# Retention and a hard-swish MLP on one core: first Q in float32 by two queues, Q columns by parity, row order in the stores, moved tile steps

## The chip, the core and the metric

The kernel runs on one core of a Trainium2 chip. The core has five engines that run their own instruction streams and wait for each other by semaphores: TensorE (PE; its weight loads are shown apart, as PEld), VectorE (DVE), ScalarE (ACT), GpSimd (POOL) and SyncE (SP). Transfers between HBM and SBUF run on 16 DMA engines; POOL, SP and ACT issue them. The metric is device time in microseconds of one execution. Before the change it is 287.6 us (median of 3 runs, 287.4 to 288.43).

## The reference

Inputs q, k, v are float32 of shape (8 batches, 8 heads, 576 tokens, 64); w_in is 512 x 2048, w_out 2048 x 512. What is computed:

```python
scores = q @ k.T / sqrt(64)                    # per batch and head
gamma  = 1 - 2 ** (-5 - h)                     # per head
D[i,j] = gamma ** (i - j) if i >= j else 0
attn   = (scores * D) @ v                      # (8, 8, 576, 64)
x      = attn as (8 * 576 tokens, 512)
h      = x @ w_in
g      = h * clip(h + 3, 0, 6) / 6
out    = g @ w_out                             # (4608, 512) float32
```

## The kernel before

Matrix products take float16 and give float32 in PSUM; loads by POOL cast float32 to float16 on the way.

The 4608 tokens are worked as 9 blocks `kb` of 512 columns. A block's columns are four pieces of 128 tokens. Pieces are ordered by position first: pieces 0 to 7 are the first 128 tokens of the eight batches, pieces 8 to 15 the next 128, and so on up to piece 31; pieces 32 to 35 hold the last 64 tokens of two batches each. So blocks 0 and 1 are all first pieces, which have no state from earlier tokens.

Pieces 0 to 7 are worked two at a time as tiles t = 0 to 3 (`first_load`, `turned`, `first_scores`, `first_out`, `first_copies`, `first_states`; L118 to L329). `first_load` puts two neighbouring tokens on one partition: partition p of a half (one batch each) holds tokens 2p and 2p+1, index `w`. `turned` transposes Q or K per parity `w` and head pair on TensorE against an identity and copies PSUM to SBUF. In the copy for Q it puts the columns back into the order of the tokens, by a strided pattern; keys stay by parity. `first_scores` multiplies K by Q, and its `mask` multiplies by `decay`, a table of decay factors made from `gap` and `behind` (L142 to L175). `first_out` multiplies with V; the result is copied to `xt`, the block's 512 columns. `first_scale` and `first_states` make the state that the next pieces of the same batch start from. All of that is called in pieces: tiles 0 and 1 at the start, 2 and 3 between the matmuls of block 0's GEMM2 and block 1's GEMM1.

Later pieces (`step4`, L757) use a running state. Their Q and K are scaled by `ahead` (L331) on DVE and then transposed by a DMA transpose that SP issues; scores of pieces 8 and 9 are the first that need one (`put_step(1, (-1, -1), [], groups[0])`, ahead of block 1's GEMM2).

Each block then has GEMM1 (`g1`, `g1_pair`: 16 chunks of 128 hidden columns, ACT and DVE apply the activation) and GEMM2. Blocks 0 and 1 use the plain form `g2` in 16 units (row group `mc`, a quarter of the sum `part`); when a row group is complete ACT copies it to `osb` and `store` (L512) sends 128 rows of 512 float32 with SP. In block 0 the order of units is by `part` first, so its four stores come close together at the end; in block 1 by `mc` first, so they are spread. Blocks 2 to 8 use `g2_seven`, seven half-size products from sums of weights (`weight_sums`, `t1` to `t4`) and sums of activations.

The order on every engine is the order in which the program is written out: no scheduler moves instructions. `put(units, steps)` runs numbered units and after unit j the steps listed under j. `load_next` issues one third (K, Q or V) of a later piece on POOL and makes it wait for the newest matmul recorded in `newest`. `warm` issues float32 matmuls on zeros in places where TensorE waits. PSUM has four shared banks (`bank`, tag `ph`) and the tags `sc`, `o` and `tu`.

SP's queue carries, in order: four stores of block 0, the transposes of pieces 8 to 13, four stores of block 1 with transposes among them, and so on.

Of the kernel before, what the change touches and what calls it, by code (L numbers as in the profile page):

```python
# [13 lines left out]
ALU = mybir.AluOpType  # L14
# [3 lines left out]
def kernel(  # L18
# [98 lines left out]

    def first_load(t, x):  # L118
        dst = first_of(t, x)
        for i in range(2):  # L120
            nc.gpsimd.dma_start(  # L121
                dst[i * HALF:i * HALF + HALF].rearrange("p h w d -> p h (w d)"),
                (q, k, v)[x][2 * t + i, :, 0:P, :].rearrange("h (p w) d -> p h (w d)", w=2))
# [10 lines left out]
    def load_wout(c0, c1):  # L134
# [31 lines left out]
    behind = const.tile([P, 2, P], FP32)  # L166
    nc.vector.tensor_scalar(out=behind, in0=gap, scalar1=0.0, scalar2=1e5, op0=ALU.is_lt,
                            op1=ALU.mult)
    nc.vector.tensor_tensor(out=behind, in0=behind, in1=gap, op=ALU.add)

# [41 lines left out]
    def warm(n, cols):  # L212

        w = psum.tile([P, MBLK], FP32, tag="tu", name=f"warm_{warmed[0]}")
# [5 lines left out]
    warm(4, MBLK // 2)  # L220

# [23 lines left out]
    def turned(t, x, copy, tag=None, ws=(0, 1)):  # L245


        src, n = first_of(t, x), len(ws)
        pt = bank_or(tag, [P, n, NPAIR, P], FP16, f"tr{'qk'[x]}_{t}_{ws[0]}")
        for i, w in enumerate(ws):  # L250
            for p in range(NPAIR):
                for h2 in range(2):
                    newest[0] = nc.tensor.transpose(pt[rows(h2), i, p, :],
                                                    src[:, 2 * p + h2, w, :], ident16)
        if x not in fst.setdefault(t, {}):
            fst[t][x] = work.tile([P, 2, NPAIR, P], FP16, tag="qk", bufs=8, name=f"t{'qk'[x]}_{t}")
        to = fst[t][x]
        if x:
            copy(to[:, ws[0]:ws[0] + n], pt)
        else:  # L260
            copy(to.rearrange("d a b c -> d (a b c)").rearrange("d (u s w) -> d w u s", w=2, s=HALF),
                 pt.rearrange("d w p (i s) -> d w (p i) s", i=2))

    def first_scores(t, w, tags=()):
        kt = fst[t][1]
        qt = fst[t][0].rearrange("d a b c -> d (a b c)").rearrange("d (p i s) -> d p i s",
                                                                   p=NPAIR, i=2)
        if tags:
# [7 lines left out]
        for p in range(NPAIR):  # L276
            for i in range(2):
                for h2 in range(2):
                    nc.tensor.matmul(banks[h2][rows(i), p, :], kt[rows(h2), w, p, rows(i)],
                                     qt[rows(h2), p, i, :], start=True, stop=True)  # L280

        def mask():
            if tags:
                for h2 in range(2):
                    nc.vector.tensor_tensor(out=at[:, h2], in0=banks[h2], in1=decay[:, w, h2],
                                            op=ALU.mult)
            else:
                nc.vector.tensor_tensor(out=at, in0=sc, in1=decay[:, w], op=ALU.mult)
# [223 lines left out]
    def store(kb, mc, cols, src):  # L512
        if kb < B:
            _, b, i, _ = pieces[PER * kb + mc]
            r0 = b * S + i * P
            nc.sync.dma_start(out[r0:r0 + P, cols], src)
        else:
# [7 lines left out]
    def g2(kb, mc, part):  # L525
# [4 lines left out]
        for fc in range(4 * part, 4 * part + 4):  # L530
            nc.tensor.matmul(pout, gt[:, fc, P * mc:P * mc + P], wout16[:, fc, :],  # L531
                             start=(fc == 0), stop=(fc == NFC - 1))
        if part == 3:
# [153 lines left out]
    for i in range(2, 4):  # L687
        load_win(i * WQ, i * WQ + WQ)
    for i in range(4):
        load_wout(4 * i, 4 * i + 4)  # L690
        if i > 1:
            for x in range(3):
                first_load(i, x)
# [7 lines left out]
    warm(1, 160)  # L701
    first_scores(0, 0)()
    turned(1, 0, by_act)
    first_scores(0, 1, (None, None))()
    warm(1, 160)
    turned(1, 1, by_act, ws=(0,))
    turned(1, 1, by_act, ws=(1,))
    warm(1, MBLK // 2)
# [94 lines left out]
    def gemm1(kb, steps):  # L803

        units = [lambda fc=fc, cols=cols: g1_pair(kb, fc, cols)
                 for cols in (lo, hi) for fc in {2: (0, 2)}.get(kb, ())]
        done = {0: 4, 1: 14, 2: 4}.get(kb, 0)
        if kb < 2:

            units = [lambda fc=fc: g1_pair(kb, fc, hi) for fc in range(0, done, 2)]  # L810
        put(units + [unit1(kb, f) for f in range(done, NFC)], steps)

    load_until(11)
    gemm1(0, {3: [(powers,)], 5: [(fill_gk2,)], 7: [(first_scale, 0), (fill_gqk, 1)],
              9: [(fill_gqk, 0)], 11: [(first_scale, 1)]})
    order = [(mc, part) for part in range(4) for mc in range(4)]
# [5 lines left out]
    def scores_of(t):  # L824
# [6 lines left out]
        {3: [(first_states, 0, 1)], 4: [(weight_sums, "t1")], 5: [(make_mask64,)],  # L831
         7: [(begin, 2), (first_scale, 2)], 10: [(scores_of, 2)], 11: [(weight_sums, "t2")],
         13: [(first_out, 2), (first_copies, 2, (by_act, by_act)),
              (weight_sums, "t3")],
         14: [(begin, 3)]})

    for fc in range(0, 14, 2):
        g1_pair(1, fc, lo)
        if fc == 0:
            scores_of(3)  # L840
        if fc == 4:
            ahead(8)
        if fc == 8:
            first_out(3)
            first_copies(3, (by_act, by_act))
            ahead(9)
            first_states(2)
        if fc > 8:
# [3 lines left out]

    within = {0: [(ahead, 10)], 4: [(ahead, 11)]}
    for j in (0, 2, 3, 5, 7, 8):
# [5 lines left out]
    groups = [[c, c + 1] for c in range(8, NP, 2)]  # L860
    steps_at = {1: {-1: [(ahead, 12)],
                    7: [(weight_sums, "t4")]}}

# [76 lines left out]
```

## Time and profile before

| | |
|---|---|
| Median of 3 runs | 287.6 us |
| Profiled execution | 287.82 us |
| Its span (first to last instruction) | 286.0 us |
| TensorE busy | 278.2 us, 97% |
| DVE busy | 228.4 us, 80% |
| ACT busy | 170.6 us, 60% |
| POOL busy | 104.3 us, 36% |
| Granted TensorE clock | 1.0 throughout |
| DMA moved | 35.72 MB, mean 125 GB/s |

How to read it: the profile is of one execution on the chip. A line of the time line gives start, duration, engine, line of the program, operation, what is written and read, and in square brackets how long the engine was idle before and what ended that. "L469" is line 469 of the kernel. A line of an answer for one source line or tile gives durations in ns as least, median and most. "DMA to landing" is the time from the issue to the last byte's semaphore. A DMA queue's line gives packets, MB, and the time its packets took as a share of 16 engines' time; q0 is POOL's queue, q1 SP's. A part that was idle on an engine that is not the bound costs nothing.

### The profile page before, as it was taken

To read this page: it belongs to the slowest core of one execution; us is meant where nothing else is said; L and a number is where in the kernel's file an instruction comes from. 1 tells how busy PE (TensorE), PEld (TensorE's weight loads), DVE (VectorE), ACT (ScalarE), POOL (GpSimd) and SP (SyncE) were. 2 spreads that over 40 slices of the span, in tenths; PEclk is the share of its full clock that TensorE was granted. 3 is DMA by queue.
4 is the path that set the end of the run, shared out by engine and by line. 5 is a ranking of instruction groups with operands and counts; after the bars stand their busy time and mean duration, and the time that the engine had idled before them with its cause. 6 is when DMAs were issued, how large, how long until landed. Compare 5 with 4: busy or idle time off the path is not lost.

```text
span 286.0 us, 9020 instructions
## 1 busy us (share of the span) xinstructions
PE 278.2 (97%) x3836; PEld 183.4 (64%) x3836; DVE 228.4 (80%) x385; ACT 170.6 (60%) x295; POOL 104.3 (36%) x136
## 2 busy tenths in 40 slices
PE   6999999999999999999999999999999999999994
PEld 4674455874465687468745974597458845874583
DVE  4577656999769998899889988998799678727871
ACT  6469316773468655875587557754875487357710
POOL 8952479159015333332543344355640000000000
PEclk9999999999999999999999999999999999999999
DMA  8999999999999998999999999989992250121014
GB/s 80 172 203 205 189 187 192 193 138 140 144 163 163 148 93 119 163 147 91 123 161 164 91 138 142 172 85 139 147 159 50 77 110 3 39 77 37 0 39 110
DMA packets 143880, 35.72 MB, mean 125 GB/s; under 512 B 130624, under 2 KB 142784, under 8 KB 143840
## 3 DMA queue, kind: packets, MB, share of 16 engines
q0 software_dynamic: 105552, 18.49, 85.2%
q1 hardware_dynamic: 37840, 16.26, 29.0%
q8 instruction: 30, 0.49, 0.7%
q10 hardware_dynamic: 448, 0.39, 0.4%
q14 instruction: 10, 0.08, 0.1%
HBM read 36.70 MB, written 9.44 MB: 161 GB/s over the span
## 4 chain that ended last, share of the span: by engine, by line
PE 78%; DMA 11%; POOL 7%; DVE 2%; issue 1%; ACT 0%; POOLq 0%
PE ph L469 33%; PE x L617 15%; PE z L617 9%; DMA wout<-in_moe_w_out_dram 9%; PE pout L531 5%; PE y L617 4%; PE ph L497 3%; DMA qkn<-in_k_dram 2%; POOL qkn L121 2%; PE o L380 2%; PE sc L348 2%; POOL win L130 2%; PE o L402 2%; POOL qkn L107 2%; PE u L430 1%; PE xtu L617 1%
## 5 line engine op out<-in xcount | busy, mean ns | idle before, releaser
L469 PE MATMUL ph<-xt,win 128*128 128x512 f16 x488 | 106.8, 379 | 0.0
L477 ACT ACTIVATE u<-ph,cb 128x512 f32<-128x512 f32 x122 | 83.4, 688 | 20.4 <-PE ph L469 20.1
L478 DVE SCALAR_TENSOR_TENSOR gt<-u,ph 128x512 f16<-128x512 f32 x122 | 81.1, 684 | 16.9 <-ACT u L477 15.6
L469 PEld LDWEIGHTS <-win 128*128 128x128 f16 x488 | 47.7, 98 | 55.7
L617 PEld LDWEIGHTS <-sum_s 128*128 128x128 f16 x448 | 43.1, 98 | 5.8 <-issue 0.6
L107 POOL DMA_DIRECT2D vn<-in_v_dram x32 | 26.7, 835 | 37.9 <-PE ph L497 14.6
L107 POOL DMA_DIRECT2D qkn<-in_k_dram x32 | 26.7, 834 | 33.1 <-PE ph L469 11.6
L617 PEld LDWEIGHTS <-gt 128*128 128x128 f16 x336 | 32.5, 98 | 5.4
L107 POOL DMA_DIRECT2D qkn<-in_q_dram x32 | 26.7, 835 | 25.2 <-PE ph L469 9.6
L531 PE MATMUL pout<-wout,gt 128*128 128x512 f16 x128 | 29.5, 380 | 0.6 <-issue 0.6
L585 POOL DMA_DIRECT2D out_dram<-osb x1 | 0.6, 617 | 68.2 <-DVE osb L638 68.2
L617 PE MATMUL x<-wsum_t,sum_s 128*128 128x256 f16 x192 | 22.9, 273 | 0.0
L531 PEld LDWEIGHTS <-gt 128*128 128x128 f16 x128 | 11.7, 98 | 14.4 <-issue 1.1
L497 PE MATMUL ph<-xt,win 128*128 128x256 f16 x176 | 20.5, 273 | 0.1
L335 DVE TENSOR_TENSOR qkn<-qkn,gqk 128x1024 f16<-128x1024 f16 x28 | 19.1, 683 | 0.0
L497 PEld LDWEIGHTS <-win 128*128 128x128 f16 x176 | 17.0, 98 | 3.1 <-issue 0.6
L572 DVE TENSOR_TENSOR sum_s<-gt 128x1024 f16<-128x1024 f16 (+1 forms) x21 | 18.1, 864 | 0.2
L354 DVE TENSOR_TENSOR at<-sc,mask 128x1024 f16<-128x1024 f32 x14 | 17.0, 1216 | 1.1 <-PE sc L348 1.1
L505 ACT ACTIVATE u<-ph,cb 128x512 f32<-128x512 f32 x22 | 15.0, 688 | 4.4 <-PE ph L497 3.7
L506 DVE SCALAR_TENSOR_TENSOR gt<-u,ph 128x512 f16<-128x512 f32 x22 | 14.3, 682 | 3.2 <-ACT u L505 3.1
L414 ACT CAST xt<-o 64x512 f16<-64x512 f32 x28 | 16.2, 580 | 0.3
L617 PE MATMUL z<-wout,sum_s 128*128 128x256 f16 x112 | 13.6, 273 | 0.3 <-issue 0.3
(108 smaller groups left out, 323.7 us busy)
## 6 DMA issues: line engine op xcount, KB each, us to landing
out_dram<-osb SPq DMA_DIRECT2D x32, 256.0 KB, 3.4
qkn<-in_q_dram POOLq DMA_DIRECT2D x32, 128.0 KB, 5.6
qkn<-in_k_dram POOLq DMA_DIRECT2D x32, 128.0 KB, 5.4
vn<-in_v_dram POOLq DMA_DIRECT2D x32, 128.0 KB, 5.3
wout<-in_moe_w_out_dram POOLq DMA_DIRECT2D x4, 512.0 KB, 14.4
win<-in_moe_w_in_dram POOLq DMA_DIRECT2D x4, 256.0 KB, 7.1
win<-in_moe_w_in_dram POOLq DMA_DIRECT2D x2, 512.0 KB, 10.6
qkn<-in_k_dram POOLq DMA_DIRECT2D x8, 64.0 KB, 3.9
```

Source lines behind the costliest of these rows:

```text
L107: loaded[c]["dma"].append(nc.gpsimd.dma_start(dst[p0:p0 + n], src[b, :, s0:s0 + n, :].rearrange("h s d -> s h d")))
L335: nc.vector.tensor_tensor(out=both, in0=both, in1=gqk, op=ALU.mult)
L354: nc.vector.tensor_tensor(out=at.rearrange("t a j p s -> t (a j p) s"), in0=sc.rearrange("t a j p s -> t (a j p) s"), in1=mask64[:, None, ...
L414: nc.scalar.copy(to[rows(h2), :, :, 1, :], o[1][rows(1 - h2)].rearrange("e j p s -> e p j s"))
L469: newest[0] = nc.tensor.matmul(ph, win16[:, dmc, P * fc:P * fc + P], xt_of(kb)[:, dmc, :], start=(dmc == 0), stop=(dmc == NCC - 1))
L477: nc.scalar.activation(u, ph, ACTF.Relu, bias=cb[:, 0:1], scale=1.0 / 6.0)
L478: nc.vector.scalar_tensor_tensor(out=gts[kb][:, fc, :], in0=u, scalar=1.0, in1=ph, op0=ALU.min, op1=ALU.mult)
L497: newest[0] = nc.tensor.matmul(ph[:, i], win16[:, dmc, P * (fc + i):P * (fc + i) + P], xt_of(kb)[:, dmc, cols], start=(i == 0 and dmc == 0 ...
L505: nc.scalar.activation(u, ph, ACTF.Relu, bias=cb[:, 0:1], scale=1.0 / 6.0)
L531: nc.tensor.matmul(pout, gt[:, fc, P * mc:P * mc + P], wout16[:, fc, :], start=(fc == 0), stop=(fc == NFC - 1))
L572: nc.vector.tensor_tensor(out=s(which)[:, c0:c1], in0=x(), in1=y(), op=op)
L617: newest[0] = nc.tensor.matmul(dst, left()[:, c, P * u:P * u + P], right[:, c, :], start=(first and c == 0 and (u == 0 or name not in whol ...
```

## The change

Five things change.

- The first tile's Q is loaded in float32 into a tile `plain` (it shares a buffer with the second activation block), one half by SP and one by ACT, and DVE copies it to float16. The other loads stay on POOL in the same order.
- `turned` copies Q as it is, by parity. Scores, outputs and `xt` of blocks 0 and 1 then have their columns in the order (parity, pair); the table `behind` is made in that order, in two halves; and `store` puts the rows back in order by its destination pattern.
- The second tile's O comes ahead of GEMM1's first pair; ACT copies one half of the last scores to SBUF before DVE multiplies; the warm-up matmuls have other sizes and places, and the two on zeros ahead of GEMM1 are gone.
- `g2` records its matmuls in `newest`, so loads issued during it wait for them.
- Steps of tiles 2 and 3 move: states of tile 2 and scores of tile 3 into block 0's GEMM2, scale and states of tile 3 into block 1's GEMM1, `t2` one unit on, `t3` into block 1's GEMM2, `t4` four units on, the first `step4` behind unit 0 of that GEMM2.

```diff
+    plain = work.tile([P, NFC // 2, MBLK], FP32, tag="gt16", bufs=2, name="plain")
+    plain_q = plain[:, 0:2].rearrange("t a (h w d) -> t (a h) w d", w=2, d=D)
+    first_load(0, 0, plain_q, (nc.sync, nc.scalar))
...
-    for t, x in ((0, 0), (0, 1), (1, 0), (1, 1), (0, 2), (1, 2)):
+    for t, x in ((0, 1), (1, 0), (1, 1), (0, 2), (1, 2)):
         first_load(t, x)
...
+    ahead_by = gap.rearrange("t a (s w) -> t a w s", w=2)
+    late = behind.rearrange("t a (w s) -> t a w s", w=2)
+    for i in range(2):
+        nc.vector.tensor_scalar(out=late[:, i], in0=ahead_by[:, i], scalar1=0.0, scalar2=1e5,
+                                op0=ALU.is_lt, op1=ALU.mult)
+        nc.vector.tensor_tensor(out=late[:, i], in0=late[:, i], in1=ahead_by[:, i], op=ALU.add)
...
-        if x:
-            copy(to[:, ws[0]:ws[0] + n], pt)
-        else:
-            copy(to.rearrange("d a b c -> d (a b c)").rearrange("d (u s w) -> d w u s", w=2, s=HALF),
-                 pt.rearrange("d w p (i s) -> d w (p i) s", i=2))
+        copy(to[:, ws[0]:ws[0] + n], pt)
...
-            nc.sync.dma_start(out[r0:r0 + P, cols], src)
+            nc.sync.dma_start(out[r0:r0 + P, cols].rearrange("(s w) n -> w s n", w=2), src)
...
-            nc.tensor.matmul(pout, gt[:, fc, P * mc:P * mc + P], wout16[:, fc, :],
-                             start=(fc == 0), stop=(fc == NFC - 1))
+            newest[0] = nc.tensor.matmul(pout, gt[:, fc, P * mc:P * mc + P], wout16[:, fc, :],
+                                         start=(fc == 0), stop=(fc == NFC - 1))
...
+    by_dve(first_of(0, 0), plain_q)
     turned(0, 0, by_dve)
-    warm(1, MBLK // 2)
     turned(0, 1, by_act, ws=(0,))
     turned(0, 1, by_act, ws=(1,))
...
     masks[1] = first_scores(1, 0)
+    warm(1, 80)
+    masks[2] = first_scores(1, 1, (None, None), (1,))
     first_out(0)
-    masks[1]()
-    masks[1] = first_scores(1, 1, (None, None))
+    masks.pop(1)()
+    masks.pop(2)()
     first_copies(0, (by_act, by_act))
-    masks[1]()
-    acts = [g1_pair(0, 0, lo, True, 2)]
+    warm(2, 224)
     first_out(1)
     first_copies(1, (by_act, by_dve))
-    acts.append(g1_pair(0, 2, lo, True))
+    acts = [g1_pair(0, f, cols, True) for f, cols in ((0, lo), (0, hi), (2, lo))]
...
-         7: [(begin, 2), (first_scale, 2)], 10: [(scores_of, 2)], 11: [(weight_sums, "t2")],
-         13: [(first_out, 2), (first_copies, 2, (by_act, by_act)),
-              (weight_sums, "t3")],
-         14: [(begin, 3)]})
+         7: [(begin, 2), (first_scale, 2)], 9: [(scores_of, 2)], 11: [(first_states, 2)],
+         12: [(first_out, 2), (first_copies, 2, (by_act, by_act)), (weight_sums, "t2")],
+         14: [(begin, 3)], 15: [(scores_of, 3)]})
...
-    within = {0: [(ahead, 10)], 4: [(ahead, 11)]}
+    within = {0: [(ahead, 10)], 2: [(first_scale, 3)], 4: [(ahead, 11)], 7: [(first_states, 3)]}
...
-    put_step(1, (-1, -1), [], groups[0])
-    steps_at[1][3] = [(first_scale, 3)]
-    steps_at[1][10] = [(first_states, 3)]
+    put_step(1, (0, 0), [], groups[0])
```

More of the change, by code (lines that the diff above doesn't have):

```diff
@@ L212, in warm @@
     def warm(n, cols):
-        w = psum.tile([P, MBLK], FP32, tag="tu", name=f"warm_{warmed[0]}")
+        w = bank([P, MBLK], FP32, name=f"warm_{warmed[0]}")
         warmed[0] += 1
@@ L218, in warm @@
                              start=True, stop=True)
-    warm(4, MBLK // 2)
+    warm(5, MBLK // 2)
     def make_mask64():
@@ L279, in first_scores @@
                     nc.tensor.matmul(banks[h2][rows(i), p, :], kt[rows(h2), w, p, rows(i)],
-                                     qt[rows(h2), p, i, :], start=True, stop=True)
+                                     qt[rows(h2), :, p, rows(i)], start=True, stop=True)
         def mask():
             if tags:
+                for h2 in copied:
+                    nc.scalar.copy(at[:, h2], banks[h2])
                 for h2 in range(2):
-                    nc.vector.tensor_tensor(out=at[:, h2], in0=banks[h2], in1=decay[:, w, h2],
-                                            op=ALU.mult)
+                    nc.vector.tensor_tensor(out=at[:, h2], in0=at[:, h2] if h2 in copied else banks[h2],
+                                            in1=decay[:, w, h2], op=ALU.mult)
             else:
@@ L688 @@
         load_win(i * WQ, i * WQ + WQ)
-    for i in range(4):
+    for i in range(3):
         load_wout(4 * i, 4 * i + 4)
-        if i > 1:
-            for x in range(3):
-                first_load(i, x)
+    first_load(2, 0)
+    first_load(2, 1)
+    first_load(2, 2)
+    load_wout(12, 16)
+    for x in range(3):
+        first_load(3, x)
     by_act, by_dve = nc.scalar.copy, nc.vector.tensor_copy
     masks = {}
+    by_dve(first_of(0, 0), plain_q)
     turned(0, 0, by_dve)
-    warm(1, MBLK // 2)
     turned(0, 1, by_act, ws=(0,))
     turned(0, 1, by_act, ws=(1,))
-    warm(1, 160)
+    warm(1, 112)
     first_scores(0, 0)()
@@ L846 @@
             ahead(9)
-            first_states(2)
         if fc > 8:
@@ L860 @@
     groups = [[c, c + 1] for c in range(8, NP, 2)]
-    steps_at = {1: {-1: [(ahead, 12)],
-                    7: [(weight_sums, "t4")]}}
+    steps_at = {1: {-1: [(ahead, 12)], 7: [(weight_sums, "t3")], 11: [(weight_sums, "t4")]}}
     def put_step(kb, at, ended, begun):
```

26 lines of the change are left out of this document (10 added, 16 removed).

## The prediction

> **What bounds the kernel now.** I read the page first, then busy time by stretches (length, then busy time of TensorE, its weight loads, DVE, ACT and POOL, granted clock, DMA share, GB/s), then the time line of the start, then the DMA answers for the stretch in which the first stores leave.
>
> ```profile
> span 286.0 us, 9020 instructions
> PE 278.2 (97%) x3836; PEld 183.4 (64%) x3836; DVE 228.4 (80%) x385; ACT 170.6 (60%) x295; POOL 104.3 (36%) x136
> ```
>
> ```profile
> 17.39:30.50 13.11, 13.11 (x80) 7.03 (x73) 10.12 (x16) 12.27 (x24) 4.31 (x7) 1.00 1.26 206
> 30.50:48.70 18.20, 18.20 (x257) 9.25 (x256) 11.92 (x19) 6.06 (x9) 13.89 (x18) 1.00 1.88 182
> 48.70:64.60 15.90, 15.84 (x217) 12.76 (x215) 13.97 (x24) 11.88 (x19) 6.69 (x9) 1.00 1.78 174
> ```
>
> TensorE is busy 97% of the span, and from 17.39 on it is full in every stretch: 13.11 of 13.11, 18.20 of 18.20, 15.84 of 15.90. So a start of GEMM1 that comes earlier passes to the end one for one, unless something that TensorE waits for is not earlier too. The second thing to see is the last but one column, the DMA share: on average 1.26 to 1.88 packets are in flight on each DMA engine. They are nearly full exactly where the changed stores lie.
>
> The profiled execution took 287.82 us, its span 286.0; the median of the runs is 287.6. The sum below is made against 287.82.
>
> **The start, step by step.**
>
> ```profile
> 1.36 1.53 POOL L121 DMA_DIRECT2D qkn<-in_q_dram  x2 [0.18 <-issue]
> 3.12 3.30 ACT L173 ACTIVATE decay<-behind,cb 128x256 f16<-128x256 f32 x8 [0.87 <-DVE behind L169]
> ...
> 6.30 1.06 PE L253 MATMUL trq<-ident,qkn 128*64 128x128 f16 x16 [1.33 <-DMA qkn<-in_q_dram]
> 7.40 1.31 DVE L261 COPY tq<-trq 128x1024 f16<-128x1024 f16 x1 [3.14 <-PE trq L253]
> 8.45 1.06 PE L253 MATMUL trk<-ident,qkn 128*64 128x128 f16 x16
> 10.27 0.61 PE L279 MATMUL sc<-tq,tk 64*64 64x128 f16 x16
> 10.81 0.64 PE L253 MATMUL trq<-ident,qkn 128*64 128x128 f16 x16
> 11.01 1.22 DVE L288 TENSOR_TENSOR at<-sc,decay 128x1024 f16<-128x1024 f32 x1 [2.30 <-PE sc L279]
> 12.16 1.28 DVE L285 TENSOR_TENSOR at<-sc,decay 128x512 f16<-128x512 f32 x2
> 16.82 0.64 PE L300 MATMUL o<-at,vn 64*64 64x128 f16 x32
> 17.39 2.85 PE L497 MATMUL ph<-xt,win 128*128 128x256 f16 x23
> ```
>
> ```profile
> 39.42 0.69 DVE L259 COPY tk<-trk 128x1024 f16<-128x1024 f16 x1 [1.49 <-PE trk L253]
> ```
>
> ```profile
> L130 POOL DMA_DIRECT2D win<-in_moe_w_in_dram x1: 883/883/883, 9.6 to 9.6; - x1
> ...
> DMA to landing us min/median/max: 6.0/6.0/6.0
> ```
>
> ```profile
> out_dram<-osb SPq DMA_DIRECT2D x3, 128.0 KB, 2.6
> ```
>
> First Q: two issues leave POOL (1.53 us), one each goes to SP and ACT; everything behind on POOL (K, V, win, wout) is issued 1.5 us sooner, in the same order. On ACT the issue stands ahead of the table load and the exponentials, which wait for `behind` until 3.12 anyway. `behind` in four instructions instead of two: between 0 and +0.4 us on DVE, I take 0.2, hidden until ACT's 3.30 us of exponentials end (about 6.7). No row shows a load by SP or ACT. Bounds for Q's arrival: 1.36 + 2.6 = 4.0 (the nearest row of that queue, a 128 KB store, lands in 2.6 us; SP is taken to issue no later than POOL does now), and 6.3, where Q arrives now. I take 5, the middle, since twice the bytes are written. New is a copy of 128x1024 on DVE, between 0.69 (`tk` by DVE, the same size in 16 bit) and 1.31 (the copy of `tq`); I take 1.0, again the middle, so transposes of Q from about 6.0. DVE waits for Q there, and the copies and masks of tile 0 queue behind that wait; none of them could start before K.
>
> K now holds Q's old place, and lands at about 6.4. Its 16 transposes (1.06 us, slow clock) run without the warm-up between, ACT's copies follow, and the first scores start at about 8.2 instead of 10.27. The copy of `tq` is plain, 0.69 instead of 1.31. Then DVE holds the pace: masks 1.22 + 1.28 + 1.22, and for the last half of 1.28 and about 0.4 (an estimate: half of 0.69 and a start), because ACT takes one half: 4.8 us from 8.7, when the scores end, gives 13.5, second O 0.64, GEMM1 from 14.2. The first 256 columns of win (9.6 + 6.0 = 15.6 now) minus 1.5 are there at 14.1, and V, issued ahead of them in the same queue, before. At 17.39 before, 72 of GEMM1's 80 matmuls were left; now all 80 are, 8 x 2.85 / 23 = 1.0 us more. Gain 17.39 - (14.2 + 1.0) = 2.2 us. Both ends: 0 (Q as late as now plus the copy) and 3.0 (Q at 4.0; then masks, V and win hold). The new warm-up matmuls and the two removed on zeros lie in TensorE waits: nothing.
>
> **The moved work of tiles 2 and 3.** Scores of tile 3 go from block 1's GEMM1 into block 0's GEMM2, states of tile 2 there too, states of tile 3 from GEMM2 into GEMM1, `t2`, `t3` later on DVE, the first group step behind one unit. TensorE's sum does not change (every instruction is there in both), and DVE is busy 11.92 of 18.20 and 13.97 of 15.90 in these stretches, so a weight sum less in the first and the scale and states of tile 3 more in the second (0.69 + 0.75, rows below) fit; without that cover the first masks of GEMM2 would be late by that 1.4. Loads in block 1's GEMM2 now wait for its matmuls, where they had only the last matmul of GEMM1 to wait for; they come later, at no price that I take.
>
> ```profile
> 70.94 0.69 DVE L236 TENSOR_TENSOR qkn<-qkn,gk 128x1024 f16<-128x1024 f16 x1
> ...
> 73.95 3.20 PE L531 MATMUL pout<-wout,gt 128*128 128x512 f16 x14 [0.61 <-issue]
> 77.59 0.75 DVE L329 TENSOR_TENSOR ts<-u,gc 128x256 f16<-128x256 f32 x2 [0.32 <-PE u L318]
> ```
>
> Taken: 0, bounds -0.6 (the one TensorE gap there, 0.61 us ahead of 73.95, goes) and +1.4.
>
> **The stores, where I differ from "nothing".** In the built program the eight stores of blocks 0 and 1 change from a destination of 128x512 to one of 2x64x512; the source stays 128x512. Bytes and rows of 2 KB are the same. What changes is by what the transfer can be shared out. Now:
>
> ```profile
> L516 SPq DMA_DIRECT2D out_dram<-osb x8: 332/332/524, 45.1 to 84.9; - x8
> ...
> DMA to landing us min/median/max: 2.1/6.0/8.9
> ```
>
> ```profile
> q1 hardware_dynamic: 144, 0.26, 38.0%
> ```
>
> The first is all eight stores: 2.1 us at best (the last one, with next to no loads beside it), 6.0 in the middle. The second is the DMA answer for 85 to 87, with that last store: 128 packets of 2 KB (and 16 small ones) took 0.38 x 16 x 2 us = 12.2 us in all, 95 ns each. It lands in 2.1 us, so it runs on all 16 engines, 8 packets each; on two it would need 64 x 95 ns = 6.1 us. Equal shares along the first dimension fit this. With a first dimension of 2 on one side there are two shares, and SP's whole 256 KB goes through two engines. Every transfer in this trace has 64 or 128 rows first, so no row decides it; that shares follow the first dimension is what I lean on, at 0.72. The Trainium skill says the same in "DMA: Bandwidth & Descriptors", section "Why a DMA increments its semaphore by 16 and not by 1": the number of engines is the largest up to 16 that divides the slowest dimension of both sides; by it k is 2 here. No run here shows k under 16 yet; by the rows of 128 alone the sum would be 285.4, by the rule it is the forecast.
>
> What it costs. On the two engines each block's four stores are 256 packets, 24.3 us alone. They share the engines with the loads, and behind them in SP's queue stand the transposes of Q and K:
>
> ```profile
> q0 software_dynamic: 5609, 0.71, 187.8%
> ```
>
> ```profile
> q0 software_dynamic: 2866, 0.36, 154.5%
> q1 hardware_dynamic: 297, 0.54, 39.3%
> ```
>
> ```profile
> 45.13 4.72 SPq L516 DMA_DIRECT2D out_dram<-osb  x4
> ```
>
> ```profile
> DMA to landing us min/median/max: 3.2/3.2/3.2
> ```
>
> ```profile
> 64.88 0.46 PE L348 MATMUL sc<-qk 64*64 64x64 f16 x32
> ```
>
> The first row is the loads from 45 to 51, the pair after it 47.3 to 51.0, stores and loads together: per engine 179 load packets and 17.6 of 2 KB in 3.7 us, so one store packet per 10 of loads and 0.21 us. After the change the first store leaves at 45.13 - 2.2 + 0.4 = 43.3 (states of tile 2 now stand ahead). The landing line is that of the one transpose issued from 55 to 56, alone in the queue. The transposes of pieces 8 and 9 are wanted at 64.88 - 2.2 + 0.4 + 0.9 = 64.0, one unit and one set of states later. Until then 20 thirds of loads (K, Q or V of a piece) cross the engines, 12 of pieces 8 to 11 and 8 more by the program's order, each 128 KB in packets of 128 bytes, 64 per engine: 1280. Lower end: stores alone, 43.3 + 1.3 + 24.3 + 2 for the transposes = 70.9, TensorE stands 7 us. Upper end: loads in full beside them at 17 ns (5609 packets, 16 engines and 6 us give the same), 22 us more: 29 us. By the shared rate: 1280 loads carry 128 store packets in 27 us, the other 128 take 12: 43.3 + 1.3 + 27 + 12 + 2 = 85.6. I take 20, the row with both queues being the nearest.
>
> Block 1's stores do it again, against 26.7 us from the first store to the first use of piece 14:
>
> ```profile
> 73.03 12.20 SPq L516 DMA_DIRECT2D out_dram<-osb  x4
> ```
>
> ```profile
> 99.69 0.50 PE L348 MATMUL sc<-qk 64*64 64x64 f16 x32
> ```
>
> Alone 24.3 + 1.3 + 2 = 27.6, a stall of 1; with 13 load thirds in full, 14 more: 15. Taken 6. After waits this long TensorE restarts slow (the 16 transposes took 1.06 at 6.30, 0.64 at 10.81): about 4 us of work at 0.6 speed, +2 in all; bounds 0 and 4.
>
> Sum: 287.82 - 2.2 + 20 + 6 + 2 = 313.6, rounded to 313. Ends: 287.8 - 3.0 - 0.6 + 7 + 1 = 292 and 287.8 + 1.4 + 29 + 15 + 4 = 337. Against the median it is 0.2 less, which is inside the rounding.
>
> **Rivals.**
> - Stores on 16 engines all the same: then only the start counts, 287.82 - 2.2 - 0.2 (part of the gap at 73.95) = 285.4. For it: 0.3 us issues and 2.1 us landing of the same bytes; against it, the first dimension of 2. It decides if a store of block 0 still lands within 7 us under loads. Chance 0.21. This is the other side.
> - Stores on 16 engines, and Q by SP and ACT no sooner than by POOL: trq at 6.3 + 1.0, scores at about 10, the gain shrinks to what the plain copy and ACT's half mask give, 0.4 us: 287.4. For it: no load by these queues has a row; against it, POOL's own first issue starts only at 1.36. Chance 0.07.
> - Stores on two engines, but the transposes do not stand behind them (the engine alternates between transfers of one queue): only loads are slower, 20 thirds of 64 packets at 21 instead of 17 ns, 5 us: 290.6. For it: the shared rate above is between queues; against it, one queue, in order of issue. Chance 0.10.
> - As forecast: 0.62.
>
> **The numbers.** Half a per cent, 1.4 us, is about what a measurement can tell from no change. Slower by more than that: 0.62 + 0.10 = 0.72. Within: 0.07. Faster: 0.21. The forecast alone ranges from 292 to 337. For eight in ten the range must take in part of the fast rivals: 285 to 328 leaves out about one in ten below and as much above.
>
> **What will show it.** Stores of blocks 0 and 1 landing in 10 to 30 us instead of 2.1 to 8.9, and only two engines' shares pending; the first transposes of Q and K landing around 80 instead of 59; TensorE idle at the scores of pieces 8 and 9 with a DMA as releaser. The start is right if the first scores begin near 8.2 and GEMM1 runs unbroken from about 14.2. The forecast falls if these stores land as before.

## The result and the profile after

The changed kernel takes 321.56 us (median of 4 runs, 320.2 to 322.65) against 288.0 for the kernel before (4 runs, 287.4 to 288.43): a ratio of 1.1165, 95% interval 1.111 to 1.1219. The profiled execution took 320.2 us, its span is 318.4. A few executions of a kernel are slower as a whole (one of the form with two copies took 724.61 us, for a reason that stays open), and the medians and ratios below leave them out.

The page of the changed kernel, its span, TensorE's busy time and the granted clock in 40 slices:

```profile
span 318.4 us, 9035 instructions
PE 283.7 (89%) x3838; PEld 185.3 (58%) x3838; DVE 228.5 (72%) x388; ACT 170.0 (53%) x296; POOL 103.2 (32%) x134
PEclk9999999965599985799999999999999999999999
```

The span is 32.4 us longer. TensorE's idle time went from 286.0 - 278.2 = 7.8 to 318.4 - 283.7 = 34.7, which is 26.9 of it; its busy time rose by 5.5, with nearly the same matmuls, because the granted clock falls around two places. Both places are seen in the stretches (length, busy time of TensorE, its weight loads, DVE, ACT, POOL, granted clock, DMA share, GB/s), first of the changed kernel, then of the one before:

```profile
62.00:100.00 38.00, 23.60 (x427) 11.39 (x425) 16.67 (x31) 8.90 (x19) 8.51 (x10) 0.73 1.68 96
100.00:130.00 30.00, 17.80 (x91) 9.54 (x89) 14.38 (x23) 11.74 (x19) 6.37 (x9) 0.79 1.58 91
```

```profile
62.00:100.00 38.00, 37.30 (x624) 21.02 (x623) 32.49 (x56) 22.40 (x40) 14.87 (x17) 1.00 1.68 152
100.00:130.00 30.00, 30.00 (x492) 20.61 (x479) 27.51 (x46) 19.12 (x34) 10.49 (x12) 1.00 1.25 128
```

TensorE loses 13.7 us more in the first stretch and 12.2 in the second: 25.9 of the 26.9. What it waits for, by the changed kernel's waits (total, times, longest, in us), of TensorE and then of DVE:

```profile
PE pout L534 <- DVE gt L509: 12.4, 1, 12.4
PE ph L472 <- DVE gt L481: 10.5, 1, 10.5
PE sc L351 <- DMA qk<-qkn: 2.0, 1, 2.0
PE x L620 <- DVE gt L481: 1.7, 1, 1.7
...
DVE qkn L338 <- DMA qkn<-in_q_dram: 32.1, 5, 13.4
```

The two long waits name VectorE, not a DMA. But VectorE is not slow (228.5 us busy, as before): it stands 32.1 us itself, at line 338, the scaling of a later piece in `ahead`, until that piece's load has landed. The time line shows the chain at both places:

```profile
75.03 0.69 DVE L338 TENSOR_TENSOR qkn<-qkn,gqk 128x1024 f16<-128x1024 f16 x1 [13.42 <-DMA qkn<-in_q_dram]
75.64 1.28 DVE L509 SCALAR_TENSOR_TENSOR gt<-u,ph 128x512 f16<-128x512 f32 x2
76.37 1.86 PE L534 MATMUL pout<-wout,gt 128*128 128x512 f16 x4 [12.36 <-DVE gt L509]
...
81.06 0.43 PE L351 MATMUL sc<-qk 64*64 64x64 f16 x16 [2.05 <-DMA qk<-qkn]
...
121.16 0.69 DVE L338 TENSOR_TENSOR qkn<-qkn,gqk 128x1024 f16<-128x1024 f16 x1 [12.85 <-DMA qkn<-in_q_dram]
122.51 3.57 PE L472 MATMUL ph<-xt,win 128*128 128x512 f16 x8 [10.46 <-DVE gt L481]
```

VectorE takes its instructions in order. The step of piece 11 waits 13.42 us for its load; behind it stand two halves of an activation; GEMM2 waits 12.36 us for the first of them. This is the first wait behind block 0's stores, but not the one that ends last: at 81.06 TensorE stands again, for the DMA transpose of piece 9. VectorE had scaled piece 9 at 54.68, so this transpose does not hang on piece 11's load, and TensorE could not have passed 81.06 even if VectorE had been on time (the run with the stores on ScalarE's queue, below, bears this out). So behind block 0's stores late transposes set the end; behind block 1's it is the wait for VectorE, and by it for the load of piece 16.

The loads of pieces that POOL issues (line 107) from 44 to 60 us are late, least, median and longest time to landing, in the changed kernel:

```profile
DMA to landing us min/median/max: 5.7/25.1/30.1
```

and in the kernel before:

```profile
DMA to landing us min/median/max: 4.7/7.3/8.4
```

And this is what the 16 DMA engines do from 62 to 75 us in the changed kernel (each digit of the first row is the time of the packets that begin in a fortieth of the stretch, as a mean share of the 16 engines, in tenths; then packets and MB of SP's queue and the time that these packets took, as a share of 16 engines' time):

```profile
DMA  1111111399999911111111111111111111111499
...
q1 hardware_dynamic: 938, 0.64, 96.6%
```

For most of 13 us the mean share is a tenth, which is what two of 16 engines make (0.125). From 53 to 56 us SP's queue has almost nothing but store packets in it, and they take 11.4% of 16 engines' time, 1.8 engines:

```profile
q1 hardware_dynamic: 59, 0.12, 11.4%
```

The 512 store packets of block 0 follow each other at this pace from 46.92 to 73.98, 27 us, where the kernel before needs 8 (47.26 to 55.21). The digits from 66.3 us on hide something: 27 packets, 19 of a transpose and 8 of a load, begin at 65.9 to 66.3, take 8.0 to 8.5 us each, and all end at 74.3 to 74.4, right behind the last store packet. Most of the 96.6% is these. No packet of the kernel before took over 1.5 us between 38 and 130 us. So loads and transposes alike wait until the stores are through two engines: piece 11's load is there at 75.03, piece 9's transpose at 81.06.

### The profile page after: what moved, and what is told of

It is laid out like the page before. It is cut to its first block, busy times and chain, and to the rows that moved or that the text cites. A ratio compares the mean times of both kernels' runs of the same rounds, so it can differ in the third digit from the quotient of the medians.

```text
span 318.4 us, 9035 instructions
## 1 busy us (share of the span) xinstructions
PE 283.7 (89%) x3838; PEld 185.3 (58%) x3838; DVE 228.5 (72%) x388; ACT 170.0 (53%) x296; POOL 103.2 (32%) x134
## 4 chain that ended last, share of the span: by engine, by line
PE 58%; DMA 23%; POOL 9%; issue 8%; DVE 1%; ACT 0%; POOLq 0%; DVEq 0%
PE ph L472 26%; PE x L620 14%; PE z L620 8%; DMA wout<-in_moe_w_out_dram 8%; DMA qkn<-in_k_dram 8%; DMA qkn<-in_q_dram 7%; PE y L620 4%; POOL qkn L107 3%; POOL vn L107 2%; POOL win L130 1%; PE o L383 1%; POOL qkn L121 1%; PE o L405 1%; PE xtu L620 1%; PE sc L351 1%
## 5 line engine op out<-in xcount | busy, mean ns | idle before, releaser
L472 PE MATMUL ph<-xt,win 128*128 128x512 f16 x488 | 108.8, 383 | 10.5 <-DVE gt L481 10.5
L480 ACT ACTIVATE u<-ph,cb 128x512 f32<-128x512 f32 x122 | 83.0, 688 | 47.6 <-PE ph L472 19.3
L534 PE MATMUL pout<-wout,gt 128*128 128x512 f16 x128 | 32.9, 411 | 12.4 <-DVE gt L509 12.4
L107 POOL DMA_DIRECT2D qkn<-in_k_dram x32 | 26.6, 831 | 50.1 <-PE x L620 17.0
L338 DVE TENSOR_TENSOR qkn<-qkn,gqk 128x1024 f16<-128x1024 f16 x28 | 19.2, 685 | 32.1 <-DMA qkn<-in_q_dram 32.1
L107 POOL DMA_DIRECT2D vn<-in_v_dram x32 | 26.6, 833 | 39.9 <-DMA qkn<-in_k_dram 11.6
L107 POOL DMA_DIRECT2D qkn<-in_q_dram x32 | 26.6, 832 | 39.4 <-PE ph L472 15.7
L620 PEld LDWEIGHTS <-gt 128*128 128x128 f16 x336 | 33.3, 100 | 8.3 <-issue 2.5
L534 PEld LDWEIGHTS <-gt 128*128 128x128 f16 x128 | 12.5, 104 | 28.3 <-issue 16.5
L620 PE MATMUL x<-wout,gt 128*128 128x256 f16 x96 | 13.0, 295 | 1.7 <-DVE gt L481 1.7
```

The costliest lines, as they stand in the source:

```text
L107: loaded[c]["dma"].append(nc.gpsimd.dma_start(dst[p0:p0 + n], src[b, :, s0:s0 + n, :].rearrange("h s d -> s h d")))
L338: nc.vector.tensor_tensor(out=both, in0=both, in1=gqk, op=ALU.mult)
L472: newest[0] = nc.tensor.matmul(ph, win16[:, dmc, P * fc:P * fc + P], xt_of(kb)[:, dmc, :], start=(dmc == 0), stop=(dmc == NCC - 1))
L480: nc.scalar.activation(u, ph, ACTF.Relu, bias=cb[:, 0:1], scale=1.0 / 6.0)
L534: newest[0] = nc.tensor.matmul(pout, gt[:, fc, P * mc:P * mc + P], wout16[:, fc, :], start=(fc == 0), stop=(fc == NFC - 1))
L620: newest[0] = nc.tensor.matmul(dst, left()[:, c, P * u:P * u + P], right[:, c, :], start=(first and c == 0 and (u == 0 or name not in whol ...
```

## The experiments

### Stores by two copies

```diff
-            nc.sync.dma_start(out[r0:r0 + P, cols].rearrange("(s w) n -> w s n", w=2), src)
+            rows_by = out[r0:r0 + P, cols].rearrange("(s w) n -> w s n", w=2)
+            for w in range(2):
+                nc.sync.dma_start(rows_by[w], src[w * HALF:w * HALF + HALF])
```

> The changed kernel with each of the eight stores of blocks 0 and 1 cut in two by parity: two transfers of 64 rows, first dimension 64, same rows, same bytes, same queue. Theory A (a transfer is shared out by its first dimension, so 2 means two DMA engines): everything that was lost comes back, TensorE no longer waits behind DVE near 64 and 112 us, and only the start counts: 286.5 us, between 285.5 and 287.5, since GEMM1 begins about 1 us sooner in the changed kernel's trace. Theory B (a strided row order in HBM is slow by itself): still above 310. Theory C (the moved steps hold DVE, not the stores): still 320.

Measured: 287.72 us (11 runs), ratio 0.9967 (0.9942 to 0.9991), 0.2 us above the range that I had given. A second run of the same kernel gives the profile, and is the companion with which later runs are compared:

> The changed kernel with each of the eight stores issued as two copies of 64 rows, one for each parity; everything else of the change stands. The profiled execution of the first run of this form was one of some 725 us, and tells nothing of where the time lies, so the form is run again for its profile and as the companion of the next runs. Two-engine theory: 287.0 to 288.2 us, ratio 0.995 to 0.999 to the kernel before; TensorE has no wait above 2.5 us in the trace, VectorE's wait for the loads of the pieces is below 3 us in all, and the loads land in 5 to 8 us beside the stores. Rival (the parity order in the stores costs in itself, whatever the number of copies): waits of TensorE of 5 us or more stay about 85 us, and VectorE waits there for loads.

Measured: 287.32 us (286.18 to 287.97), ratio 0.9959 (0.9942 to 0.9975). Its page, its waits of TensorE and the landing of the loads issued from 44 to 60 us:

```profile
span 284.4 us, 9047 instructions
PE 276.5 (97%) x3838; PEld 183.2 (64%) x3838; DVE 228.3 (80%) x388; ACT 170.4 (60%) x296; POOL 103.4 (36%) x134
```

```profile
PE trq L259 <- DVE qkn L705: 1.3, 1, 1.3
PE warm L223 <- DVE cb L153: 1.2, 1, 1.2
```

```profile
DMA to landing us min/median/max: 6.5/7.4/8.9
```

The same bytes go to the same rows; only the transfer is cut so that each copy has 64 rows first. All 34 us are gone, with every long wait after the start. The rest of the change, taken together, costs no more than it brings.

### The kernel before with other first dimensions

```diff
-            nc.sync.dma_start(out[r0:r0 + P, cols], src)
+            nc.sync.dma_start(out[r0:r0 + P, cols].rearrange("(s w) n -> w s n", w=2), src)
```

and the same with w=4, 8 and 16.

> The kernel before with one edit: the eight stores of blocks 0 and 1 take the destination pattern with first dimension 2 (so the rows of these two blocks land in another order; no other work differs). Theory A: the whole loss without any other part of the change, 317 to 323 us, DVE waiting over 10 us for loads twice. Theory C: 288.

> As before with first dimension 4 (rows of blocks 0 and 1 in yet another order). Theory A: four engines, each store 32 packets per engine instead of 64, so 12 us of extra transfer per block in place of 24; the first wait shrinks from 14 us to about 2: 290 to 294 us. Theory B: as slow as with 2.

> The kernel before with the destination of its first stores written as 8 by 16 rows (so the rows of the first two blocks come out permuted among themselves), nothing else changed. Between the forms with a first dimension of 4 (309.77 us) and 16 (288.86 us). If what costs is the time that the stores' engines are taken, it halves from 2 to 4 to 8: eight engines with 64 packets each per store cost 5 to 12 us, 293 to 300 us. If what costs is that loads are late beyond the slack that the kernel has, the slack hides all of it: 288 to 291 us.

> As before with first dimension 16: a three-dimensional, strided destination like the changed kernel's, rows of blocks 0 and 1 in another order, but 16 shares. Theory A: no loss, 288 within 0.5 per cent. Theory B: 310 or more.

| first dimension | us | ratio to before (95%) | block 0's stores, first to last packet, us | loads issued at 44 to 60: median to landing, us |
|---|---|---|---|---|
| 128 (before) | 288 | 1 | 8.0 | 7.3 |
| 16 | 288.86 | 1.0005 (0.9982 to 1.0027) | 8.8 | 6.3 |
| 8 | 291.32 | 1.0117 (1.0038 to 1.0195) | 10.4 | 8.6 |
| 4 | 309.77 | 1.0722 (1.0674 to 1.077) | 14.7 | 19.3 |
| 2 | 322.82 | 1.1172 (1.1125 to 1.1219) | 26.2 | 24.2 |

With 4, from 60 to 63 us, the packets of SP's queue, most of their time that of stores, take 22.3% of 16 engines' time, 3.6 engines:

```profile
q1 hardware_dynamic: 144, 0.21, 22.3%
```

With 2 the kernel before has the changed kernel's loss, and the same waits of TensorE and VectorE:

```profile
PE u L430 <- DVE gt L506: 12.8, 1, 12.8
PE x L617 <- DVE gt L478: 12.5, 1, 12.5
PE sc L348 <- DMA qk<-qkn: 4.0, 2, 2.8
...
DVE qkn L335 <- DMA qkn<-in_q_dram: 33.1, 5, 13.6
```

So the moved steps and the new start have no part in it. With 16 the pattern is as strided as with 2, and costs nothing: it is the number of shares, not the pattern. With 4 the expected 290 to 294 was far off: the loss is 0.62 of that of two (7.22% of 11.72%), where I had it nearly hidden. With 8 the measured 291.32 lies between the two theories' figures and decides neither; the landing median of 8.6 says that the loads are hardly late.

### The stores on ScalarE's queue

The changed kernel, with its stores as they are but issued by ScalarE:

```diff
-            nc.sync.dma_start(out[r0:r0 + P, cols].rearrange("(s w) n -> w s n", w=2), src)
+            nc.scalar.dma_start(out[r0:r0 + P, cols].rearrange("(s w) n -> w s n", w=2), src)
```

> The changed kernel with its stores unchanged in shape (2x64x512, by two DMA engines), but issued on ScalarE's queue, so that SP's queue holds the DMA transposes alone and none of them stands behind a store. The prediction's theory (the transposes are late because they stand behind the stores in SP's queue, and that is the stall): most of the 32 us goes, 288 to 296 us. The theory that the after's trace suggests (the pieces' loads on POOL's queue share the two engines with the stores and land in 20 to 30 us; VectorE waits for them in order, and the activation's half on VectorE with it): the time stays at 314 to 322 us, VectorE's wait for the loads stays near 25 to 32 us, and only the 2 us of scores waiting for transposes goes. A third possibility is that ScalarE is held by issuing the stores, as SP's issue of one transpose took 13.0 us: then it is above 322 us, with ScalarE as releaser of TensorE's waits.

Measured: 321.85 us (2 runs), ratio 1.1177 (1.1112 to 1.1242). Its waits of TensorE and of VectorE:

```profile
PE sc L351 <- DMA qk<-qkn: 9.9, 2, 5.1
PE ph L472 <- DVE gt L481: 9.2, 1, 9.2
PE sc L280 <- ACT tq L264: 3.1, 1, 3.1
PE ph L500 <- DVE gt L509: 2.6, 1, 2.6
...
DVE qkn L338 <- DMA qkn<-in_q_dram: 24.5, 3, 11.6
```

No store stands ahead of a transpose in a queue any more, and nothing is won: the order in SP's queue is not what makes the transposes late. They are late all the same, in 13.4 us in the middle for those issued from 40 to 125 us, against 5.8 in the kernel before. That of piece 9 is issued at 62.96 and lands 18.3 us later, and TensorE gets to its scores when it did in the changed kernel (81.06):

```profile
81.27 0.43 PE L351 MATMUL sc<-qk 64*64 64x64 f16 x16 [5.11 <-DMA qk<-qkn]
```

The total agrees with the other theory, but its detail does not. VectorE's wait for piece 11's load fell from 13.42 to 3.67 us, without any gain, and the waits for transposes grew from 2.0 to 9.9 us, where I had expected them to go. Nor is the run a clean one: ScalarE, which now issues the stores (one issue took it 4.8 us), makes TensorE wait 3.1 us for a copy of Q (line 264) and, by the activation, 2.6 us more in block 1's GEMM1 (line 500).

### The moved steps put back

The form with two copies, with the steps of tiles 2 and 3 and the weight sums where the kernel before has them, and `g2` no longer recorded in `newest`, so the loads' waiting for it is undone too (the other lines of the edit are left out here):

```diff
-         7: [(begin, 2), (first_scale, 2)], 9: [(scores_of, 2)], 11: [(first_states, 2)],
-         12: [(first_out, 2), (first_copies, 2, (by_act, by_act)), (weight_sums, "t2")],
-         14: [(begin, 3)], 15: [(scores_of, 3)]})
+         7: [(begin, 2), (first_scale, 2)], 10: [(scores_of, 2)], 11: [(weight_sums, "t2")],
+         13: [(first_out, 2), (first_copies, 2, (by_act, by_act)),
+              (weight_sums, "t3")],
+         14: [(begin, 3)]})
...
-    put_step(1, (0, 0), [], groups[0])
+    put_step(1, (-1, -1), [], groups[0])
...
```

> The companion with the steps of tiles 2 and 3, the weight sums of tiles 2 to 4 and the first step of the pieces' heads put back where the kernel before has them; loads of the first tiles, start, and stores in two copies stay as changed. If the moved work is worth nothing, as the prediction has it (0, between -0.6 and +1.4 us), it is within 0.7 us of its companion: 286.9 to 288.4 us. If the moves cost or save more, it stands outside that.

Measured: 288.57 us (287.59 to 291.06), ratio 1.0006 (0.9982 to 1.003), 1.25 above its companion and outside the 0.7 that I had expected. The profiled execution can't be taken for the size of this, since it began in another way, although nothing of the start differs. Stretches of it, and then of its companion (the last but two number is the granted clock):

```profile
8.00:20.00 12.00, 11.89 (x201) 9.08 (x197) 5.98 (x8) 5.27 (x9) 9.40 (x13) 0.57 1.54 193
```

```profile
8.00:20.00 12.00, 11.59 (x219) 8.80 (x214) 7.96 (x12) 8.06 (x13) 9.49 (x14) 1.00 1.54 194
```

GEMM1's first 512-wide matmul begins at 22.86 in the one and 18.96 in the other. From there to the end it is 289.3 - 22.86 = 266.4 against 284.4 - 18.96 = 265.4, and 286.0 - 20.19 = 265.8 in the kernel before. Between these single executions the moved steps bring 0.4 to 1.0 us. The other way of beginning does not explain the medians: of the twelve runs only the profiled one has a mean granted clock of 0.982, the others have 0.99 or more, and their median is 288.55. What the moved steps and the loads' new waits bring each was not parted.

### First Q again by POOL

The form with two copies, with the first Q loaded as in the kernel before:

```diff
...
-    first_load(0, 0, plain_q, (nc.sync, nc.scalar))
-    for t, x in ((0, 1), (1, 0), (1, 1), (0, 2), (1, 2)):
+    for t, x in ((0, 0), (0, 1), (1, 0), (1, 1), (0, 2), (1, 2)):
...
-    by_dve(first_of(0, 0), plain_q)
```

> The same, but the first Q comes again in float16 by POOL's queue, ahead of the other first loads, without the float32 buffer and VectorE's copy. If the two queues are what starts the kernel sooner, this one starts 0.5 to 1 us later than its companion and ends at 288.0 to 288.7 us; if the float32 Q lands no sooner than POOL's did (turned Q in the changed kernel begins at 6.98 against 6.30 before), this one is as fast as its companion or up to 0.7 us faster: 286.9 to 287.7 us.

Measured: 288.9 us (10 runs), ratio 1.0023 (0.9987 to 1.0059), 1.6 us above its companion and a little over both expectations. Its time line:

```profile
6.15 0.64 PE L256 MATMUL trq<-ident,qkn 128*64 128x128 f16 x16 [0.42 <-DMA qkn<-in_q_dram]
8.54 0.76 PE L256 MATMUL trk<-ident,qkn 128*64 128x128 f16 x16 [1.76 <-DMA qkn<-in_k_dram]
9.93 0.64 PE L277 MATMUL sc<-tq,tk 64*64 64x128 f16 x16
```

Q is there 0.8 us sooner than by two queues (6.15 against 6.98), but K lands later, so first scores begin at 9.93 instead of 8.71, and TensorE's gap ahead of K is followed by a half clock, as in the run above. Six of its twelve executions have a mean granted clock of 0.982 or less and take 290.77 us or more; the median of the other six is 288.04, 0.7 above the companion. What the two queues bring is not the earlier Q, but K in Q's old place.

### TensorE's gap before the turned Q

Two experiments change the warm-up of the form with two copies from five to six and to four pairs of matmuls:

```diff
-    warm(5, MBLK // 2)
+    warm(6, MBLK // 2)
```

> The kernel with each store in two copies, with six pairs of warming matmuls in place of five before the first turned Q, so that TensorE is idle there for some 0.6 us and not 1.3. The traces show two kinds of start: in one the granted clock stays at 1.00, in the other it is 0.50 from 9.0 us to 19 us and the first 512-wide matmul of GEMM1 begins 3.9 us later (22.86 against 18.96). If it is the idle time before the turned Q that decides between them, this one starts in the first way in nearly all its executions: median 286.6 to 287.3 us, highest below 288.3 us. If something else decides (the chip's state, the time of day of a power window), its runs spread as those of the companion and its median is 287.3 to 287.9 us.

> The same with four pairs of warming matmuls, as the kernel before has them: TensorE is idle for some 1.9 us before the turned Q. If the idle time decides, the clock falls to 0.50 in most of its executions and the median is 289.5 to 292 us; if it does not, 287.2 to 288.2 us, as with five.

Measured with six: 287.78 us (286.46 to 288.3), ratio 0.9963 (0.9946 to 0.998). With four: 289.19 us (287.17 to 291.13), ratio 1.0018 (0.9989 to 1.0047); its twelve runs lie in two groups, six from 287.17 to 288.52 and six from 289.86 to 291.13. The turned Q in the profiled execution with six, then with four, with TensorE's idle time before it:

```profile
6.91 0.67 PE L259 MATMUL trq<-ident,qkn 128*64 128x128 f16 x16 [0.23 <-DVE qkn L705]
```

```profile
7.53 0.64 PE L259 MATMUL trq<-ident,qkn 128*64 128x128 f16 x16 [2.56 <-DVE qkn L705]
```

```profile
9.00:14.00 5.00, 4.89 (x73) 3.64 (x76) 2.51 (x3) 2.59 (x5) 5.00 (x8) 0.50 1.69 185
```

The third row is a stretch of the one with four: the clock is 0.50 behind the gap. The mean granted clock of each run tells how often: it is 0.982 or less in four of the twelve with four pairs, in none of the twelve with six, and in one of the 44 runs here that have five pairs and Q by two queues (the companion's two runs, the moved steps put back, the second O in other banks). So the longest gap gives that start more often; between five and six these runs show no difference. Both expectations on the times missed. With six the median is 287.78 and the highest 288.3, over the 286.6 to 287.3 that the gap theory gave and inside its rival's range, so what spreads the runs with five is not this gap. With four the median lies between the two ranges, and two of the upper six runs have a clock of 0.997 and 1.0, so the clock alone does not make that group.

### The second O in other banks

The form with two copies, with one line changed:

```diff
-    first_out(1)
+    first_out(1, tags=(None, None))
```

(and `first_out` takes such a tag as a bank of GEMM1's).

> The companion with the second O of tile 1 in two banks of the tag that GEMM1 uses, in place of those that tile 0's O leaves, so that it need not wait for ScalarE's copies of tile 0. If that wait (second O at 14.62 with ScalarE's copy as releaser in the changed kernel) is what keeps GEMM1 at 15.2 in place of 14.2, this one begins GEMM1 0.3 to 1 us sooner and ends that much below its companion: 286.6 to 287.4 us. If what ends last there is VectorE's or ScalarE's copy of tile 1's result, or if the banks are then missing for GEMM1's first pairs, it is within 0.2 us of its companion or up to 1 us above it.

Measured: 287.66 us (286.64 to 288.77), ratio 0.9963 (0.9945 to 0.9981). Its time line:

```profile
14.77 0.94 PE L500 MATMUL ph<-xt,win 128*128 128x256 f16 x7
16.48 2.89 PE L500 MATMUL ph<-xt,win 128*128 128x256 f16 x25 [0.77 <-issue]
19.20 1.03 PE L472 MATMUL ph<-xt,win 128*128 128x512 f16 x4
```

O and GEMM1 begin 0.5 us sooner (14.77 against 15.27), and a gap of 0.77 us opens inside GEMM1's first pairs: its first 512-wide matmul begins at 19.20 against 18.96. The wait has moved, and nothing is won.

The fastest kernels here are the change with its stores as two copies (0.4% below the kernel before, ratio 0.9959) and, no different from it within their intervals, its forms with six pairs and with the second O in other banks.

## Why the prediction was right, and where not

The forecast was 313.0 us, slower with 0.72, range 285 to 328; 321.56 came.

**Two engines: right.** The step that decided the sign, shares by the first dimension, was read from one transfer's landing time. The packets (1.8 and 3.6 engines with 2 and 4), the two copies and the series 2, 4, 8, 16 show it. The Trainium skill's rule in "DMA: Bandwidth & Descriptors", section "Why a DMA increments its semaphore by 16 and not by 1" (the number of engines is the largest up to 16 that divides the slowest dimension of both sides), agrees at 2 and at 16: a loss of 11.7% and one of nothing.

**Where TensorE would stand: in part.** The prediction had the transposes of pieces 8 and 9 landing around 80 and TensorE idle for them at their scores. The scores of piece 9 go at 81.06, and that ends the stall behind block 0's stores. But the step "behind them in SP's queue stand the transposes of Q and K" is not the reason: with the stores out of SP's queue the scores go at 81.27 and the time is the same. Transposes and loads have to come through the same two engines. Nor is it the wait that TensorE meets first. It is idle 12.36 us for VectorE and only 2.05 us at the scores, because of the third rival's transfer, the loads, by a way that I did not price: I took a load's cost as throughput, 20 thirds of 64 packets at 21 instead of 17 ns, 5 us. But a load is not landed before its share on the two busy engines is, so each waits there (25.1 us against 7.3), and VectorE stands in order for it with activation halves behind. Behind block 0's stores that way lies inside the wait for the transposes; behind block 1's it is the whole wait, and the transposes of piece 14, for which I had summed, are not waited for at all.

**Its size.** Block 0: 20 forecast; 12.36 + 2.05 us of waits in the trace. Block 1: 6 forecast; 10.46 + 1.74. Together 26 against 26.6. The total is right by luck, by two errors that cancel. Block 0's stores were through in 27 us and not in the 39 of the shared rate, and the transpose then took 7 more and not 2. The second block has nothing like the slack that I gave it, because the loads of its pieces are late by then, which my sum (from its first store to the first use of piece 14) left out.

**The clock: too small.** +2 forecast, bounds 0 and 4. TensorE's busy time rose 5.5 us, with a granted clock of 0.73 and 0.79 over 38 and 30 us. The groups of GEMM2's matmuls in blocks 0 and 1, changed kernel and then form with two copies (busy time, mean ns of one), hold 3.4 of it:

```profile
L534 PE MATMUL pout<-wout,gt 128*128 128x512 f16 x128 | 32.9, 411 | 12.4 <-DVE gt L509 12.4
```

```profile
L536 PE MATMUL pout<-wout,gt 128*128 128x512 f16 x128 | 29.5, 380 | 0.0
```

**The start: half.** A gain of 2.2 us was forecast. The first 512-wide matmul of GEMM1 came from 20.19 to 19.07, 1.1 us. The changed kernel's time line:

```profile
6.23 0.69 DVE L703 CAST qkn<-plain 128x1024 f16<-128x1024 f32 x1 [1.74 <-DMA plain<-in_q_dram]
6.98 0.64 PE L259 MATMUL trq<-ident,qkn 128*64 128x128 f16 x16 [1.68 <-DVE qkn L703]
8.63 0.42 PE L280 MATMUL sc<-tq,tk 64*64 64x128 f16 x16
14.62 0.64 PE L303 MATMUL o<-at,vn 64*64 64x128 f16 x31 [0.28 <-ACT xt L310]
15.19 0.94 PE L500 MATMUL ph<-xt,win 128*128 128x256 f16 x7
16.34 2.89 PE L500 MATMUL ph<-xt,win 128*128 128x256 f16 x25 [0.22 <-issue]
```

Q came to VectorE at 6.2 and not at 5, near the late bound of 6.3; the copy took 0.69 instead of 1.0, and the transposes of Q and K 0.64 each, not the 1.06 of the kernel before that I had carried over for K; scores began at 8.63 instead of 8.2. The other 0.6 is lost later: second O waits for ScalarE's copies of tile 0, which I had given no time, and GEMM1 began at 15.19, not 14.2, with a gap at 16.34.

**The moved steps: 0 forecast, bounds -0.6 and +1.4; 0.4 to 1.0 us less measured** between single executions and 1.25 between medians, beyond my bound. The 0.61 us gap that I named as the possible gain is not in the profile with two copies; with the steps put back it is there again, 0.7 us.

**The first rival, stores on 16 engines, was priced 285.4.** The form with two copies is that case; its profiled execution took 286.18 us, the least of its nine. The start, sized 2.2 where 1.2 came, is more than the 0.8 us between them. By the medians it is 287.32 against 288.47, a gain of 1.15 us where that rival had 2.4.

**The sum.** It gave 25.8 us more than the kernel before; the profiled executions differ by 32.4. Of the 6.6 that are missing 3.5 are the clock, 1.1 the start and 0.6 the waits; 1.4 I can't place.

Open: how much of block 1's loss is VectorE's order alone. In block 0 it is nothing, as the transposes end last there. In block 1, whether VectorE's scaling of later pieces, put further back in its queue, would let TensorE run on, or whether the loads would then be late for the scores, was not tried. Why four engines lose 0.62 of what two lose, and not half or less, is open too.

## What to carry to other kernels

A rearranged view in a store can change by how many DMA engines it is carried: look at its first dimension, keep it a multiple of 16 (16, 64 and 128 lost nothing here), and cut the transfer into two if it can't be. A transfer on few engines is paid for by all others, since those land only when their share on the busy engines has. The wait is then shown at whichever in-order engine stands for them, so follow a "waits for VectorE" one step further before blaming VectorE, and look for a later wait in the same place that would have held anyway. A gap of some 2.6 us in TensorE's work near the start let the clock fall in a third of the runs; closing a gap of 1.3 us further brought nothing that could be measured.

## What was not expected

- The granted clock can halve behind a short gap. In the profiled executions it went to 0.50 from about 9 us to 19 us after idle times of 1.76 us (Q by POOL, steps put back) and 2.56 us (four pairs); after 0.23, 1.32 and 1.68 us (six pairs, two copies, the changed kernel) it stayed at 1.00. The price is 3.9 us of start (22.86 against 18.96). The Trainium skill, "TensorE: Matmul & The Clock Gate", Part 1, has the clock halved after an idle window of about 3.4 us of a free-running count. No gap here was that long, so what sets these starts stays open.
- An issue can hold a sequencer. One DMA transpose of the changed kernel took SP 13.0 us (the row has ns), behind the stores on two engines:

```profile
L339 SPq DMA_TRANSPOSE qk<-qkn x1: 13002/13002/13002, 57.4 to 57.4; - x1
```

- A float32 load of 256 KB by SP or ACT landed in 5.4 and 3.8 us, and VectorE's copy to float16 of 128x1024 took 0.69, as long as one from 16 bit.
